# A linear recurrence with two expert mixtures: the recurrence's maskings and scalings regrouped, the masked logits on another engine

## The chip, the cores and the metric

The kernel runs on one core of a Trainium2 chip. The metric is the time of one execution in microseconds (us). The core has five engines that work side by side: TensorE (PE, matrix products; its weight loads are listed as PEld), VectorE (DVE), ScalarE (ACT), GpSimd (POOL) and SyncE (SP, which here only issues DMAs). They wait for each other by semaphores.

## The reference

Three stages follow each other. The first is a recurrence over 768 positions for 4 batches and 8 heads of 48 elements:

```python
for t in range(S):
    cur = einsum('bhd,bhe->bhde', u[None] * k[:, :, t], v[:, :, t])
    y[:, :, t] = einsum('bhd,bhde->bhe', r[:, :, t], state + cur)
    state = w[None, :, :, None] * state + einsum('bhd,bhe->bhde', k[:, :, t], v[:, :, t])
```

The second is a mixture of 8 experts over the 3072 rows of 384. Rows whose product with w_skip isn't positive pass unchanged; the others choose the expert of the largest logit, go through its two layers with a ReLU between, and are added to, weighted by the softmax of the chosen logit. The third is a soft mixture: every row has 32 logits (one per slot); a softmax over all rows gives each slot its input, each of 8 experts works on four slots, and a softmax over the slots mixes the results back into the rows.

## The kernel before

The recurrence is done in chunks. A tile is 128 positions of one batch, all 8 heads; there are 24 tiles, tile j being chunk j // 4 of batch j % 4. Heads are kept in pairs: four pairs on the free dimension, the two heads of a pair on partitions 0 to 47 and 64 to 111, hence tiles of 112 partitions by 4 x 128 columns. Tables of decays, prt for r and pkt for k (the same table read backwards), scale r and k, so that one product of the scaled k and r gives the scores within the tile; a mask leaves the past, and the diagonal (the bonus u) is put in separately.

The engines' order is written out by hand: what stands in the program is the order on each engine. A loop over i = 0 to 23 holds, in this order, scores(i), state(i-1), amask(i-1), inter(i-1), stateb(i-1), trx(i-2), prep(i+1), prepk(i+1), upd(i), bonus(i), av(i-1), and pieces of the routing between them:

- prep(j) (L612): VectorE scales r (L616) and k (L618), GpSimd makes the product pd of r and k (L620). prepk(j): GpSimd scales k for the state, kt (L626).
- scores(j): TensorE makes the scores sc (L635) and the diagonal's values dt (L638); ScalarE copies dt. bonus(j): TensorE transposes them to dtk (L657).
- state(j): GpSimd multiplies the old state by the decay, tmp (L668), VectorE adds TensorE's update up (L669). stateb(j): ScalarE spreads the state for use (L677).
- past(j) (L679): VectorE multiplies the two halves of sc (one head of each pair) by the mask (L683). amask(j) (L685): VectorE puts the diagonal into both halves, at (L691).
- inter(j): TensorE adds the state's part (L703); av(j): the scores' part (L713), ScalarE copies it to yt (L716). trx(j): TensorE transposes yt, ScalarE copies it to x (L723).
- load(j): SyncE issues r and k for the buffer rkb, and k and v for kvt, three tiles ahead.

Routing goes in groups of four tiles: GR has five groups of four, then groups of two, one and one tile. route1 makes the logits (L745), route2 transposes them, route2b and choose find the chosen expert: m is 1 for a row that is computed, oh marks the expert, and mb is 0 or 65536 (L835, L796), so that rows that pass unchanged get a place out of bounds. route3 sums up, on TensorE, the places, from eb2 (the expert's number), the counts so far (ohacc) and oh; places turns them into idx (L877). scat(j) is GpSimd's indirect DMA of one tile's rows to their places in xs_d (L891); one follows in each step from i = 8 on. route4 (L897) comes in the steps i = 8, 12, 16 and 20, behind prep and count: GpSimd copies the slots' logits to lt (L903), VectorE makes the masked ones, ltm = m * NEG + logits (L904), their maximum over the group (L906), and the maximum so far, cmax (L907). In step 21, cmax is spread for the transposition that gives the maximum of each slot over the first 16 tiles (fourfold).

The first mixture starts on gathered rows when every scatter has landed. It and the second mixture aren't touched by the change. pools: rs has three buffers, ks two, at two, pd two, sc two (PSUM), the tile of dtk one, that of up one.

Of the kernel before, what the change touches and what calls it, by code (L numbers as in the profile page):

```python
# [8 lines left out]
F32 = mybir.dt.float32  # L9
# [3 lines left out]
AF = mybir.ActivationFunctionType  # L13
ALU = mybir.AluOpType
# [24 lines left out]
class Banks:  # L39
    """PSUM tiles by role: role -> [(pool, tag, bufs)], taken in turn."""  # L40
# [12 lines left out]
class Views:  # L53
    """Tiles cut out of one flat tile whose own contents are no longer needed."""
# [53 lines left out]
class Weighted:  # L108
    """Sums of the rows weighted per slot, four tiles at a time: [(quarter, slot), columns]."""
# [24 lines left out]
def slots(nc, cn, nm, pp, tag, dsb, ss):  # L134
    """Slot inputs (transposed) and, on every partition, the slots' sums: [128, 4, 32]."""
    sib = pp.tile([P, 4, 32], F32, tag=tag, name=f"sib{nm}")
    for k in range(3):
        nc.tensor.matmul(sib[:, k, :], dsb[:, k * P : (k + 1) * P], cn["sel4"], start=(k == 0), stop=False)
    nc.tensor.matmul(sib[:, 3, :], cn["onesf"], ss, start=False, stop=True)
    return sib  # L140
# [16 lines left out]
class Rows:  # L157
    """The outputs of the slots come on four rows each, (hi | hi | lo | lo): row 32 j + 8 q + s has slot 8 j + s."""
# [19 lines left out]
# pieces of the second mixture's weights, in the order of their use: half an expert's v1, or 128 rows of v2 of four experts  # L178
# [76 lines left out]
def weights(nc, lp, ez, lt, p, cx=None):  # L255
    """The combine weights of chunks 2p and 2p + 1, columns (hi | lo | hi | lo) of eight slots each."""
# [67 lines left out]
def general(tc, cn, dp, r_in, k_in, v_in, w_in, u_in, wcn, phi, w1, w2, v1, v2, out):  # L324
# [142 lines left out]
def tile_main(ctx, tc, rk, kv, wu, wcat, phi, w1, w2, v1, v2, r_in, k_in, v_in, w_in, u_in, wcn, out, dbg=None, force=False):  # L467
# [21 lines left out]
    def warm(pool, tag, n):  # L489
        """Keeps the tensor engine busy, so that its clock is up when the work arrives."""  # L490
# [48 lines left out]
    nc.vector.tensor_scalar(eb2, eb_i, 1.0 / (E * P), None, op0=ALU.mult)  # L539
# [26 lines left out]
    nc.vector.memset(cmax, NEG)  # L566
# [21 lines left out]
    prt = kp.tile([PR, 4, P], F32, name="prt")  # L588
    nc.vector.tensor_mul(prt, pt[:, :, 0:P], iw.to_broadcast([PR, 4, P]))
    pkt = prt[:, :, ::-1]  # L590
    pktok = kp.tile([P, H, D], F32, name="pktok")

    def decays():
        """The decays of k, token-major."""
# [17 lines left out]
    def prep(j):  # L612
        t = T[j]
        rkt = t["rk"]
        t["rs"] = wk.tile([PR, 4, P], F32, tag="rs", bufs=3, name=f"rs{j}")
        nc.vector.tensor_mul(t["rs"], rkt[:, 0], prt)  # L616
        t["ks"] = wk.tile([PR, 4, P], F32, tag="ks", name=f"ks{j}")
        nc.vector.tensor_mul(t["ks"], rkt[:, 1], pkt)  # L618
# [60 lines left out]
    def past(j):  # L679
        t = T[j]  # L680
        at = t["at"] = wk.tile([P, 2, 4, P], F32, tag="at", name=f"at{j}")
        for hf in range(2):
            nc.vector.tensor_mul(at[:, hf], t["sc"][:, hf], mask.rearrange("s (o t) -> s o t", o=1).to_broadcast([P, 4, P]))  # L683

    def amask(j):  # L685
# [4 lines left out]
        for hf in range(2):  # L690
            nc.vector.copy_predicated(  # L691
                at[:, hf],
                ident_i.rearrange("s (o t) -> s o t", o=1).to_broadcast([P, 4, P]),
                t["dtk"].rearrange("s (p r) -> s p r", r=32)[:, :, hf : hf + 1].to_broadcast([P, 4, P]),
            )
# [34 lines left out]
    # maxima of the slots' logits over the groups of tiles: on every row, and a slot per partition  # L730
# [17 lines left out]
    # what the last eight tiles' groups leave behind  # L748
# [10 lines left out]
    def direct(g, tag):  # L759
        """Logits of one tile, token-major at once."""  # L760
# [9 lines left out]
    def choose(g, src):  # L770
        """The choice of one tile's tokens, step by step, by way of fewer steps than several tiles take."""
# [22 lines left out]
        yield  # L794
        mb = r["mb"] = rt.tile([P, 1, 1], F32, tag="mb", name=f"mb{g}")
        nc.vector.tensor_scalar(mb, m, -65536.0, 65536.0, op0=ALU.mult, op1=ALU.add)  # L796
# [16 lines left out]
    def route2b(g):  # L813
# [20 lines left out]
        mb = r["mb"] = rt.tile([P, nb, 1], F32, tag="mb", name=f"mb{c}")  # L834
        nc.vector.tensor_scalar(mb, m, -65536.0, 65536.0, op0=ALU.mult, op1=ALU.add)  # L835
# [32 lines left out]
    def places(g):  # L868
# [8 lines left out]
        nc.vector.tensor_add(idx[:, j0 : j0 + nb].rearrange("t (b o) -> t b o", o=1), sl, r["mb"])  # L877
# [20 lines left out]
    def route4(g):  # L898
# [5 lines left out]
        nc.vector.scalar_tensor_tensor(ltm[:, j0 : j0 + nb, :], m.to_broadcast([P, nb, 32]), NEG, lg[:, :, 9:41], op0=ALU.mult, op1=ALU.add)  # L904
        cm = rt.tile([P, 32], F32, tag="cm", name=f"cm{c}")
        nc.vector.tensor_reduce(cm, ltm[:, j0 : j0 + nb, :].rearrange("t b s -> t s b"), axis=AX.X, op=ALU.max)  # L906
        nc.vector.tensor_max(cmax, cmax, cm)  # L907
# [12 lines left out]
    class Group:  # L920
        """Maximum, exponentials and weighted sums of some tiles, in pieces for the steps' gaps."""
# [50 lines left out]
    if True:  # L972
        for i in range(NT):
# [24 lines left out]
            if i == 21:  # L998
                c4t = fourfold(nc, "t", rt, cmax)
# [73 lines left out]
        weave("ccgcpgcpgccpcc", c=choose(6, "lg"), g=gates(5), p=places(5))  # L1073
# [11 lines left out]
        weave("gggccpcpcpcccc", c=choose(7, "lgp"), g=gates(6), p=places(6))  # L1085
# [27 lines left out]
        # tokens per expert, and how many decays are within bounds  # L1113
# [36 lines left out]
    def mm1(n):  # L1150
# [3 lines left out]
        # the products that need the rows' low parts come last  # L1154
# [392 lines left out]
```

## Time and profile before

| | us |
|---|---|
| median of 3 runs | 395.06 |
| lowest and highest | 393.02, 395.08 |
| span of the profiled execution | 399.5 |

The profile gives the span of its execution, from the first to the last instruction, and no other time of it. Busy time over the span: TensorE 356.0 us (89%), VectorE 279.8 (70%), ScalarE 157.4 (39%), GpSimd 124.9 (31%). A line of a timeline has the start in us from the span's start, the duration in us, the engine, the line of the kernel, the operation, what it writes and reads (partitions x elements), how many neighbours were put together (x2), and in brackets how long the engine had been idle and what ended that. An operation of VectorE that waits for something other than a semaphore is shown as busy, so it is only seen by its length. The granted clock is a share of the full 2.4 GHz; at 0.50 it is at 1.2 GHz.

### The profile page before, as it was taken

The numbers are of one execution on the slowest core, as the hardware profiler recorded it, in microseconds if no ns is written. First come the engines' busy times: TensorE is split into PE (matmuls) and PEld (weight loads), VectorE is DVE, ScalarE is ACT, GpSimd is POOL, SyncE is SP. The second block draws the span as 40 slices with busy tenths as digits, with TensorE's granted clock in tenths as the row PEclk, the third lists the DMA queues.
The fourth block names the chain that finished last, engine by engine and source line by source line (L and its number), as shares of the span: only waits on it lengthen the run. The fifth ranks groups of instructions, "written<-read, shape, count | busy, mean of one in ns | idle before, by whom it ended". The sixth has DMA issues, their size and how long they took to land. (4 is left out here: it accounts for less than half of the span.)

```text
span 399.5 us, 8463 instructions
## 1 busy us (share of the span) xinstructions
PE 356.0 (89%) x3291; PEld 286.5 (72%) x3291; DVE 279.8 (70%) x588; ACT 157.4 (39%) x337; POOL 124.9 (31%) x147
## 2 busy tenths in 40 slices
PE   6888997997979959889999999999999999999560
PEld 2676785685756837727999999999899999734250
DVE  8899799599896996664757575757575865426360
ACT  1223442242433413344546555555465652321170
POOL 7846538367684350532002020202020202010000
PEclk9668997899998979959999999999999999999895
DMA  6999768497953410128795968787877357669575
GB/s 170 254 318 244 177 190 236 114 292 180 278 160 97 121 40 2 40 88 308 254 328 200 323 213 311 223 295 239 274 256 262 117 208 244 233 216 286 174 280 203
DMA packets 46049, 84.32 MB, mean 211 GB/s; under 512 B 4361, under 2 KB 27119, under 8 KB 46000
## 3 DMA queue, kind: packets, MB, share of 16 engines
q1 hardware_dynamic: 42336, 78.68, 63.5%
q0 software_dynamic: 2720, 4.89, 4.2%
q8 instruction: 28, 0.46, 0.5%
q10 hardware_dynamic: 944, 0.12, 0.3%
q14 instruction: 21, 0.17, 0.1%
HBM read 72.88 MB, written 13.30 MB: 216 GB/s over the span
## 5 line engine op out<-in xcount | busy, mean ns | idle before, releaser
L1157 PE MATMUL hp<-xhl,wa 128*128 128x256 f32 x192 | 48.6, 290 | 0.2 <-ACT xhl L1147 0.2
L1158 PE MATMUL hp<-xhl,wa 128*128 128x256 f32 x192 | 47.2, 282 | 0.0
L953 DVE TENSOR_TENSOR wa<-w,wa 128x768 fp32r<-128x768 f32 x32 | 30.6, 955 | 22.1 <-ACT wa L965 20.9
L1182 PE MATMUL yp<-wb,hh 128*128 128x384 f32 x128 | 45.3, 354 | 0.0
L1183 PE MATMUL yp<-wb,hh 128*128 128x384 f32 x128 | 43.1, 337 | 0.0
L1184 PE MATMUL yp<-wb,hlo 128*128 128x384 f32 x128 | 43.1, 337 | 0.0
L620 POOL TENSOR_TENSOR pd<-rkb 112x512 f32<-112x512 f32 x24 | 32.5, 1352 | 32.8 <-PE dt L638 20.2
L1215 POOL DMA_INDIRECT lt_d<-lsr,id x16 | 17.5, 1097 | 80.2 <-ACT xhl L1147 56.7
L891 POOL DMA_INDIRECT xs_d<-x,idx x24 | 26.1, 1087 | 37.5 <-ACT x L723 17.6
L1157 PEld LDWEIGHTS hp<-xhl,wa 128*128 128x128 f32 x192 | 36.4, 189 | 0.5 <-ACT xhl L1147 0.5
L1158 PEld LDWEIGHTS hp<-xhl,wa 128*128 128x128 f32 x192 | 36.5, 190 | 0.0
L635 PEld LDWEIGHTS sc<-rs,ks 48*128 48x128 f32 x384 | 25.0, 199 | 15.9 <-DVE ks L618 9.6
L635 PE MATMUL sc<-rs,ks 48*128 48x128 f32 x384 | 29.8, 298 | 6.7 <-DVE ks L618 6.7
L953 DVE TENSOR_TENSOR wb<-w,wb 128x768 fp32r<-128x768 f32 x32 | 30.6, 955 | 3.1 <-ACT wb L965 3.1
L691 DVE COPY_PREDICATED at<-ident,dtk 128x512 f32<-128x512 int32 x48 | 31.8, 715 | 0.0
L683 DVE TENSOR_TENSOR at<-sc,mask 128x512 f32<-128x512 f32 x48 | 30.6, 678 | 1.5 <-PE sc L635 1.5
L1168 DVE SCALAR_TENSOR_TENSOR hlo<-hp,hh 128x512 fp32r<-128x512 f32 x32 | 22.0, 688 | 12.4 <-ACT hh L1167 12.4
L713 PE MATMUL yp<-at,kvt 128*48 128x128 f32 (+1 forms) x384 | 30.7, 310 | 0.0
L965 ACT CAST wb<-w 128x768 fp32r<-128x768 f32 x32 | 26.8, 837 | 9.0 <-PE yp L1184 5.1
L1167 ACT ACTIVATE hh<-hp 128x512 fp32r<-128x512 f32 x32 | 19.1, 598 | 26.2 <-PE hp L1160 26.2
L1160 PE MATMUL hp<-xhl,wa 128*128 128x256 f32 x192 | 28.3, 283 | 0.0
L716 ACT COPY yt<-yp 112x512 f32<-112x512 f32 x24 | 14.0, 585 | 33.1 <-PE yp L713 33.1
(320 smaller groups left out, 747.6 us busy)
## 6 DMA issues: line engine op xcount, KB each, us to landing
w<-in_w_dram SPq DMA_DIRECT2D x32, 768.0 KB
v<-in_v_dram SPq DMA_DIRECT2D x29, 768.0 KB
rkb<-in_rk_dram SPq DMA_DIRECT2D x48, 192.0 KB
kvt<-in_kv_dram SPq DMA_DIRECT2D x24, 384.0 KB
out_dram<-ob SPq DMA_DIRECT2D x5, 768.0 KB
xs_d<-zt SPq DMA_DIRECT2D x1, 3096.0 KB
xg<-xs_d POOLq DMA_DIRECT2D x6, 387.0 KB, 4.5
x<-in_v_dram SPq DMA_DIRECT2D x2, 768.0 KB
```

What stands on the lines that cost most here:

```text
L620: nc.gpsimd.tensor_mul(t["pd"], rkt[:, 0], rkt[:, 1])
L635: nc.tensor.matmul(sc[:, hf, p, :], ks[r0 : r0 + D, p, :], rs[r0 : r0 + D, p, :], start=True, stop=True)
L683: nc.vector.tensor_mul(at[:, hf], t["sc"][:, hf], mask.rearrange("s (o t) -> s o t", o=1).to_broadcast([P, 4, P]))
L691: nc.vector.copy_predicated(at[:, hf], ident_i.rearrange("s (o t) -> s o t", o=1).to_broadcast([P, 4, P]), t["dtk"].rearrange("s (p r) -> ...
L713: nc.tensor.matmul(yp[64 * hf : 64 * hf + m, p, :], kvt[:, 1, h * D : h * D + m], at[:, hf, p, :], start=(c == 0 and p == 0), stop=(p == 3))
L953: nc.vector.tensor_sub(lv, sl, hv.bitcast(F32))
L1157: nc.tensor.matmul(hp[:, f, :], hi[:, k, fs], xh[:, k, :], start=(k == 0 and f == 0), stop=False)
L1158: nc.tensor.matmul(hp[:, f, :], lo[:, k, fs], xh[:, k, :], start=False, stop=False)
L1160: nc.tensor.matmul(hp[:, f, :], hi[:, k, fs], xl[:, k, :], start=False, stop=(k == 2 and f == 1))
L1182: nc.tensor.matmul(YP[e][bl], hh[:, f, bs], hi[:, f, :], start=st, stop=False)
L1183: nc.tensor.matmul(YP[e][bl], hh[:, f, bs], lo[:, f, :], start=False, stop=False)
L1184: nc.tensor.matmul(YP[e][bl], hlo[:, f, bs], hi[:, f, :], start=False, stop=en)
```

## The change

Five things are done otherwise:

- The masked logits are made by ScalarE: one scaling of m by NEG for the group, and for each of its four tiles an addition of a bias per row. The group's maximum and the running maximum go; in step 21 VectorE takes one maximum over the 16 tiles.
- The tables prt and pkt stand in one tile, prk (the reversed one is copied there once), and one VectorE operation scales r and k, into one tile with three buffers.
- The mask is one VectorE operation over both halves, and so is the diagonal.
- mb goes: eb2 has the expert's number on partition 0 and -65536 / 8 on partition 32, which the product with a matrix of 8 adds to each chosen place; places then adds 65536 to all.
- The orders of the two weaves at the end have one step less for it; cmax needs no initial value.

The core of the diff (removed comments, empty lines and the steps of the weaves left out):

```diff
@@ constants
-    nc.vector.tensor_scalar(eb2, eb_i, 1.0 / (E * P), None, op0=ALU.mult)
+    nc.gpsimd.memset(eb2, 0.0)
+    nc.vector.tensor_scalar(eb2[0:1], eb_i[0:1], 1.0 / E, None, op0=ALU.mult)
+    nc.vector.memset(eb2[32:33], -float(NOROW // E))
-    nc.vector.memset(cmax, NEG)
@@ decay tables
-    prt = kp.tile([PR, 4, P], F32, name="prt")
+    prk = kp.tile([PR, 2, 4, P], F32, name="prk")
+    prt, pkt = prk[:, 0], prk[:, 1]
     nc.vector.tensor_mul(prt, pt[:, :, 0:P], iw.to_broadcast([PR, 4, P]))
-    pkt = prt[:, :, ::-1]
+    nc.vector.tensor_copy(pkt, prt[:, :, ::-1])
@@ def prep(j)
-        t["rs"] = wk.tile([PR, 4, P], F32, tag="rs", bufs=3, name=f"rs{j}")
-        nc.vector.tensor_mul(t["rs"], rkt[:, 0], prt)
-        t["ks"] = wk.tile([PR, 4, P], F32, tag="ks", name=f"ks{j}")
-        nc.vector.tensor_mul(t["ks"], rkt[:, 1], pkt)
+        rks = wk.tile([PR, 2, 4, P], F32, tag="rks", bufs=3, name=f"rks{j}")
+        t["rs"], t["ks"] = rks[:, 0], rks[:, 1]
+        nc.vector.tensor_mul(rks, rkt, prk)
@@ def past(j)
-        for hf in range(2):
-            nc.vector.tensor_mul(at[:, hf], t["sc"][:, hf], mask.rearrange("s (o t) -> s o t", o=1).to_broadcast([P, 4, P]))
+        nc.vector.tensor_mul(at, t["sc"], mask.rearrange("s (a o t) -> s a o t", a=1, o=1).to_broadcast([P, 2, 4, P]))
@@ def amask(j)
-        for hf in range(2):
-            nc.vector.copy_predicated(
-                at[:, hf],
-                ident_i.rearrange("s (o t) -> s o t", o=1).to_broadcast([P, 4, P]),
-                t["dtk"].rearrange("s (p r) -> s p r", r=32)[:, :, hf : hf + 1].to_broadcast([P, 4, P]),
-            )
+        nc.vector.copy_predicated(
+            at,
+            ident_i.rearrange("s (a o t) -> s a o t", a=1, o=1).to_broadcast([P, 2, 4, P]),
+            t["dtk"].rearrange("s (p o r) -> s r p o", o=1, r=32)[:, 0:2].to_broadcast([P, 2, 4, P]),
+        )
@@ choose, route2b
-        nc.vector.tensor_scalar(mb, m, -65536.0, 65536.0, op0=ALU.mult, op1=ALU.add)
@@ def places(g)
-        nc.vector.tensor_add(idx[:, j0 : j0 + nb].rearrange("t (b o) -> t b o", o=1), sl, r["mb"])
+        nc.vector.tensor_scalar(idx[:, j0 : j0 + nb].rearrange("t (b o) -> t b o", o=1), sl, float(NOROW), None, op0=ALU.add)
@@ def route4(g)
-        nc.vector.scalar_tensor_tensor(ltm[:, j0 : j0 + nb, :], m.to_broadcast([P, nb, 32]), NEG, lg[:, :, 9:41], op0=ALU.mult, op1=ALU.add)
-        cm = rt.tile([P, 32], F32, tag="cm", name=f"cm{c}")
-        nc.vector.tensor_reduce(cm, ltm[:, j0 : j0 + nb, :].rearrange("t b s -> t s b"), axis=AX.X, op=ALU.max)
-        nc.vector.tensor_max(cmax, cmax, cm)
+        mn = rt.tile([P, nb, 1], F32, tag="mn", name=f"mn{c}")
+        nc.scalar.mul(mn, m, NEG)
+        for b in range(nb):
+            nc.scalar.activation(ltm[:, j0 + b, :], lg[:, b, 9:41], AF.Identity, bias=mn[:, b, :])
@@ the loop over i
             if i == 21:
+                nc.vector.tensor_reduce(cmax, ltm[:, 0:16, :].rearrange("t b s -> t s b"), axis=AX.X, op=ALU.max)
                 c4t = fourfold(nc, "t", rt, cmax)
```

## Rows read from the trace of the kernel before

**Rows 1.** Busy time by window: us, TensorE, loads, VectorE, ScalarE, GpSimd, clock, DMA, GB/s.

```profile
20.00:30.00 10.00, 8.91 (x102) 7.21 (x103) 10.00 (x14) 2.54 (x7) 4.92 (x5) 0.66 1.04 317
67.00:70.00 3.00, 3.00 (x21) 2.19 (x22) 3.00 (x6) 0.59 (x1) 1.78 (x2) 0.50 0.46 113
200.00:300.00 100.00, 100.00 (x734) 95.64 (x733) 63.80 (x103) 54.63 (x103) 16.18 (x20) 1.00 0.79 266
```

**Rows 2.** Timeline of TensorE, recurrence: start, us, line, operation, count, idle before, releaser.

```profile
38.14 1.20 PE L635 MATMUL sc<-rs,ks 48*128 48x128 f32 x16
...
44.65 1.16 PE L635 MATMUL sc<-rs,ks 48*128 48x128 f32 x16
...
60.17 1.16 PE L635 MATMUL sc<-rs,ks 48*128 48x128 f32 x16
...
66.76 0.47 PE L657 MATMUL dtk<-ident,dts 128*128 128x128 f32 x1 [1.77 <-DVE at L691]
...
72.45 1.16 PE L635 MATMUL sc<-rs,ks 48*128 48x128 f32 x16
...
87.95 1.16 PE L635 MATMUL sc<-rs,ks 48*128 48x128 f32 x16
...
97.38 1.16 PE L635 MATMUL sc<-rs,ks 48*128 48x128 f32 x16
...
112.88 1.16 PE L635 MATMUL sc<-rs,ks 48*128 48x128 f32 x16
...
124.01 1.16 PE L635 MATMUL sc<-rs,ks 48*128 48x128 f32 x16
...
138.85 1.16 PE L635 MATMUL sc<-rs,ks 48*128 48x128 f32 x16
...
146.19 0.47 PE L657 MATMUL dtk<-ident,dts 128*128 128x128 f32 x1 [4.39 <-DVE at L691]
...
151.53 1.16 PE L635 MATMUL sc<-rs,ks 48*128 48x128 f32 x16
```

**Rows 3.** Timeline of VectorE from 59 to 66 us.

```profile
59.43 3.65 DVE L904 SCALAR_TENSOR_TENSOR ltt<-m,lg 128x128 f32<-128x128 f32 x1
...
63.92 0.34 DVE L669 TENSOR_TENSOR sp<-up,tmp 112x192 f32<-112x192 f32 x1
...
64.19 1.27 DVE L683 TENSOR_TENSOR at<-sc,mask 128x512 f32<-128x512 f32 x2
...
65.39 1.32 DVE L691 COPY_PREDICATED at<-ident,dtk 128x512 f32<-128x512 int32 x2
```

**Rows 4.** Timeline of GpSimd from 58 to 63 us.

```profile
58.87 1.33 POOL L891 DMA_INDIRECT xs_d<-x,idx  x1 [3.09 <-ACT sbd L677]
...
61.94 0.99 POOL L626 TENSOR_TENSOR kt<-kvt,pktok 128x384 f32<-128x384 f32 x1
```

**Rows 5.** Timeline of VectorE behind the recurrence.

```profile
173.11 0.42 DVE L1097 SCALAR_TENSOR_TENSOR ltt<-m,lg 128x256 f32<-128x256 f32 x1
173.57 0.58 DVE L1098 TENSOR_REDUCE cmax<-ltt 128x32 f32<-128x256 f32 x1
```

**Rows 6.** Groups by line and form, ScalarE, 0 to 185 us: busy us, mean ns.

```profile
L829 ACT ACTIVATE ex<-dd 128x32 f32<-128x32 f32 x5 | 1.1, 229 | 0.9 <-DVE dd L825 0.8
```

**Rows 7.** Groups by line and form, VectorE, 0 to 170 us.

```profile
L583 DVE TENSOR_TENSOR pt<-pt 112x256 f32<-112x256 f32 x1 | 0.4, 424 | 0.0
...
L583 DVE TENSOR_TENSOR pt<-pt 112x128 f32<-112x128 f32 x1 | 0.3, 291 | 0.0
```

**Rows 8.** Timeline of VectorE, early steps.

```profile
24.23 2.71 DVE L618 TENSOR_TENSOR ks<-rkb,prt 112x512 f32<-112x512 f32 x1
```

**Rows 9.** Timeline of TensorE, early steps.

```profile
21.09 2.02 PE L635 MATMUL sc<-rs,ks 48*128 48x128 f32 x16 [2.31 <-DVE ks L618]
...
32.95 1.16 PE L635 MATMUL sc<-rs,ks 48*128 48x128 f32 x16 [1.35 <-DVE ks L618]
```

**Rows 10.** Timeline of VectorE in a step that chooses experts.

```profile
52.28 1.11 DVE L835 TENSOR_SCALAR mb<-m 128x4 f32<-128x4 f32 x1
```

More of the change, by code (lines that the diff above doesn't have):

```diff
@@ L794, in choose @@
         yield
-        mb = r["mb"] = rt.tile([P, 1, 1], F32, tag="mb", name=f"mb{g}")
-        nc.vector.tensor_scalar(mb, m, -65536.0, 65536.0, op0=ALU.mult, op1=ALU.add)
-        yield
         oh = r["oh"] = rtile(g, "oh", oh8, BF16)
@@ L833, in route2b @@
         nc.vector.tensor_reduce(m2, t8, axis=AX.X, op=ALU.max)
-        mb = r["mb"] = rt.tile([P, nb, 1], F32, tag="mb", name=f"mb{c}")
-        nc.vector.tensor_scalar(mb, m, -65536.0, 65536.0, op0=ALU.mult, op1=ALU.add)
         oh = r["oh"] = rtile(g, "oh", oh8, BF16)
@@ L1072, in tile_main @@
         route3(5, "t", (4,))
-        weave("ccgcpgcpgccpcc", c=choose(6, "lg"), g=gates(5), p=places(5))
+        weave("ccgcpgcpgcpcc", c=choose(6, "lg"), g=gates(5), p=places(5))
         for j in range(20, 22):
@@ L1084, in tile_main @@
         trx(23, "tp", pc)
-        weave("gggccpcpcpcccc", c=choose(7, "lgp"), g=gates(6), p=places(6))
+        weave("gggccpcpcpccc", c=choose(7, "lgp"), g=gates(6), p=places(6))
         nc.scalar.copy(RT[7]["lg"], RT[7]["lgp"][:, :, 0:42])
```

## The prediction

> **What bounds the kernel now.** I read the stages first (busy time by window, [rows 1]), then TensorE's timeline through the recurrence [rows 2], and then, for each hole in it, VectorE's timeline [rows 3] and GpSimd's [rows 4] at the same moment. The chain of waits on the page has one piece and says nothing here. From 200 to 300 us TensorE is busy for all 100 us at full clock (the first mixture): nothing that this change touches is in there, so whatever the recurrence gives is a plain shift of that stage. In the recurrence (about 9 to 170 us) VectorE fills whole windows, 10.00 of 10.00 us from 20 to 30, where the granted clock is 0.66, that is partly at the lower of its two levels (1.2 GHz).
>
> [rows 2] gives the step from one tile's scores to the next. Every fourth step also carries the logits of a group. Where nothing disturbs it, at 38.14 to 44.65, such a step takes 6.51 us. The three steps after it take 60.17 - 44.65 = 15.52, or 5.17 each. The next fourth steps take 72.45 - 60.17 = 12.28, 97.38 - 87.95 = 9.43, 124.01 - 112.88 = 11.13 and 151.53 - 138.85 = 12.68 us. These four are where the time is lost. At 66.76 TensorE has waited 1.77 us for VectorE's diagonal (L691), at 146.19 it has waited 4.39; and behind the first hole the clock is down to 0.50 (67 to 70 us, [rows 1]), the lower level, so that the products after it take twice as long.
>
> The cause stands in [rows 3] and [rows 4]. At the end of each group, route4 masks the logits on VectorE (L904). That operation starts at 59.43 and lasts 3.65 us; with the maximum and the running maximum behind it (L906, L907), VectorE gets to the state update only at 63.92, 4.49 us later. The same operation at twice the width, 128x256, takes 0.42 us at 173.11 [rows 5], behind GpSimd's last product. So it isn't work, it is a wait: GpSimd begins a scatter at 58.87 and runs without a gap to the end of the kt product, 61.94 + 0.99 = 62.93, and L904 ends 0.15 us behind that. The Trainium skill, "SBUF — State Buffer", section "Who interferes with whom", has a VectorE instruction with two SBUF inputs and a GpSimd instruction that reads SBUF exclude each other, for the length of one instruction. By that rule L904 would have waited for the scatter alone, 1.33 us, and taking it away would be worth about 1 us a group; the trace shows the wait through four GpSimd operations in a row, and I go by the trace.
>
> **Part 1, the masked logits.** Four times, L904, L906 and L907 go: 4.49 us of VectorE at the first. In their place ScalarE does one small scaling and four additions with a bias per row, 128x32 each. The nearest row is the exponential of 128x32, 0.23 us [rows 6]; five in a train are 0.9 to 1.3 us. They stand behind ScalarE's copy of x and ahead of its copy of yt, which waits for TensorE then; their inputs were made a step earlier. If that cover were gone they would put off yt by at most 1.3 us, which the logits' products would see. I cost them at 0. (The Trainium skill, "ScalarE: Activation LUTs", section "Rules for kernel authors", speaks against the move: additions and products belong on VectorE, which is faster per element. By it the sum would be a loss of some 1 us of ScalarE a group; here what matters is who waits for GpSimd, and the 0.23 us of [rows 6] hold no such wait.) With the wait gone, what is late next? The state update needs GpSimd's tmp product, which lies behind the scatter, between 60.20 and 61.94: VectorE goes on near 60.8 (an estimate) rather than 63.92, 3.1 us earlier. Mask (1.20 us, from 64.19 to 65.39) and diagonal (as much) then end near 63.3, when TensorE has just come to the transposition that waited until 66.76. So the hole closes, and with it the loss of clock. The first three fourth steps become 6.51 us: 5.77 + 2.92 + 4.62 = 13.3 us.
>
> **The fourth of them is different.** Here the one maximum over 16 tiles stands ahead of the mask on VectorE, and waits for ScalarE's last addition. In place of the first group's 4.49 us stand a wait of about 1.0 us for the additions and a maximum of 128x512 of about 1.0 us (0.58 at 128x256, [rows 5], in proportion to columns less a fixed part): 2.5 us earlier. If the clock stays up as well it is more; 12.68 - 6.51 = 6.2 is the most. If the copy behind the maximum (SBUF to SBUF, no row shows it beside GpSimd) waits as long as L904 did, some 3.4 us, nothing is left. I take 3.8, between 2.5 and 6.2, since the clock was down behind the first hole as well; ends 0 and 6.2.
>
> **Part 2, r and k scaling in one operation, mask and diagonal in one each.** Work saved: for a product of two tensors 256 columns cost 0.424 and 128 cost 0.291 us [rows 7], so 1.04 ns a column and 0.16 fixed, of which neighbours overlap about half: 0.06 to 0.08 us per merged pair, three pairs a step, 0.2 us. Where TensorE sets the pace that is worth nothing; between 12 and 40 us, where VectorE does, 6 steps, 1.2 us. More comes from the waits. The scaling of r and k has two SBUF inputs. The scaling of k at 24.23 takes 2.71 us [rows 8] for what is some 0.65 of work (half of the pair at 64.19, [rows 3]): it waits for GpSimd, while that of r, just ahead, got in. One operation can wait once, not twice, and starts where r's started. Against that, it holds GpSimd for twice as long, and the products pd and kt start up to 0.6 us later; they are needed a step later. TensorE waited 2.31 us for the scaling at 21.09 and 1.35 at 32.95 [rows 9], with the clock down in between. Bounds: 0 (each wait only moves) to 4.5 us (both holes and the merges). Above that the DMA would set the pace: its share is 1.04 from 20 to 30 us [rows 1], so the r and k of later tiles can't land much earlier. I take 3.0, nearest to the two holes less one wait that stays.
>
> **Part 3, small ones.** The copy of the reversed decay table adds an operation of 112x512 ahead of the first scaling: 0.3 to 0.7 us, partly beside the wait for GpSimd's first product: 0.3 lost. The constant row for the slot (mb) goes; at 52.28 it takes 1.11 us [rows 10], again a wait for GpSimd. The next operation with two SBUF inputs is the merged scaling, which takes that wait over: 0, at most 1.0 a group. And in the three closed holes the merged scaling comes at about 63.3, when GpSimd has ended kt (62.93) and goes on to the next scatter: if it is caught behind a run of GpSimd as L904 was, the next scores are late by some 1.3 us. I take 0.8 for all of that, at most 4.5.
>
> **Sum.** 13.3 + 3.8 + 3.0 - 0.3 - 0.8 = 19.0 us. The profile gives its execution's span, 399.5 us, and no time apart from it; the median of the runs is 395.06, 1.1% less, which would make 19.0 into 18.8. I subtract 19.0 from the median: 376.0 us.
>
> **Rivals.** (a) *The wait moves rather than goes.* The merged scaling inherits it at all four ends of groups and in the early steps: 13.3 - 4.5 + 0 + 0 - 0.3 = 8.5 us, 386.5 us. For it: the scaling is the next operation with two SBUF inputs, and GpSimd has the same work to do. Against it: in the closed holes it comes 3 us ahead of need. (b) *Slower: the wait comes in every step.* The merged scaling is long, GpSimd is late by it, runs without gaps to catch up, and so catches the next scaling. VectorE's work of a step is 1.20 + 1.20 + 1.2 + 0.3 (63.92 to 64.19) = 3.9 us against 5.17 of TensorE, so up to 1.27 us of waiting a step is hidden; from there it decides. With 3.4 us, as L904's, in each of the 12 steps from 60.17 to 138.85: (3.4 - 1.27) x 12 = 25.6 lost against 19.0 won, 401.7 us. Against it: GpSimd has gaps in most steps now. (c) *No change*: the shift is given back before the first mixture, for instance if the gathered rows wait for something that isn't moved: within 2 us of 395. Against it: the scatters follow the steps. (d) *More than I count*: the clock stays up from the first scores on, and 6.2 in the fourth: 13.3 + 6.2 + 4.5 = 24.0, 371.0 us.
>
> **Numbers.** My forecast with its own bounds 0.73, (a) 0.13, (d) 0.07, (c) 0.03, (b) 0.04. The range that holds 8 in 10 goes from (d)'s 371.0 to 384.0, between the forecast and (a). A measurement of this kernel can tell about 0.5% (2 us) from no change; so faster 0.93, same 0.03, slower 0.04.
>
> **What would show it.** Right: no VectorE operation of route4 left; the four fourth steps at 6.5, 6.5, 6.5 and under 10 us; TensorE's clock at 1.00 from 60 to 125 us; ScalarE's additions of 0.2 to 0.3 us, done before yt's copy would wait; the first mixture starting 17 to 21 us earlier with its own length unchanged. Wrong: merged scalings of over 1.3 us (a wait on GpSimd) in more than a few steps, GpSimd's pd or kt stretched so that TensorE waits for them, TensorE waiting for ScalarE's yt, or a diagonal or mask that costs more per column merged than split.

## The result and the profile after

| | before | after |
|---|---|---|
| median, us | 395.07 (4 runs) | 380.75 (4 runs) |
| lowest and highest, us | 393.02, 398.72 | 379.41, 381.62 |
| span of the profiled execution, us | 399.5 | 379.9 |
| ratio of the times, 95% interval | | 0.9654, 0.9604 to 0.9705 |

The change makes the kernel 14.3 us faster by the medians; 19.0 was forecast (376.0 us, measured 380.75, inside the range of 371.0 to 384.0). The spans differ by 19.6, which looks like the sum of the prediction and isn't, as the part on the reasons shows. Three executions, one of before (811.8 us), one of e5 (535.33) and one of e11 (811.76), took far longer than all the others, and the ratios leave such slow ones out.

TensorE's timeline through the recurrence, of the kernel after; columns as in [rows 2], whose steps these lines answer:

```profile
35.90 1.16 PE L636 MATMUL sc<-rks 48*128 48x128 f32 x16
42.37 1.16 PE L636 MATMUL sc<-rks 48*128 48x128 f32 x16
47.71 1.16 PE L636 MATMUL sc<-rks 48*128 48x128 f32 x16
...
50.75 0.43 PE L639 MATMUL dt<-pd,usel 112*32 112x128 f32 x8 [1.87 <-DVE lg L814]
...
56.23 1.16 PE L636 MATMUL sc<-rks 48*128 48x128 f32 x16
60.98 1.16 PE L636 MATMUL sc<-rks 48*128 48x128 f32 x16
67.45 1.16 PE L636 MATMUL sc<-rks 48*128 48x128 f32 x16
...
83.04 1.16 PE L636 MATMUL sc<-rks 48*128 48x128 f32 x16
89.51 1.16 PE L636 MATMUL sc<-rks 48*128 48x128 f32 x16
...
105.63 1.16 PE L636 MATMUL sc<-rks 48*128 48x128 f32 x16
113.68 1.16 PE L636 MATMUL sc<-rks 48*128 48x128 f32 x16 [1.18 <-DVE rks L619]
...
128.80 1.16 PE L636 MATMUL sc<-rks 48*128 48x128 f32 x16
136.88 1.16 PE L636 MATMUL sc<-rks 48*128 48x128 f32 x16
```

The fourth steps are 6.47, 6.47, 8.05 and 8.08 us, where [rows 2] gives 12.28, 9.43, 11.13 and 12.68: the four holes are gone or halved. There is another hole in an ordinary step: from tile 7's scores at 47.71 to tile 8's at 56.23 (called step 7 to 8 from here on) it takes 8.52 us, where the profile of before that the prediction read has 5.43. It isn't the change's own: a second profile of before has it too (e0).

Busy time by window, kernel after (columns as in [rows 1]):

```profile
51.00:54.70 3.70, 3.70 (x36) 3.24 (x28) 2.67 (x6) 1.56 (x5) 1.26 (x1) 0.54 0.38 80
67.00:70.00 3.00, 3.00 (x38) 2.23 (x35) 2.90 (x3) 0.85 (x2) 2.81 (x3) 1.00 1.04 250
200.00:300.00 100.00, 100.00 (x732) 95.64 (x731) 65.14 (x108) 54.76 (x104) 16.08 (x20) 1.00 0.75 251
```

From 67 to 70 us the granted clock is 1.00, not 0.50 as in [rows 1]. The clock now falls behind the hole of step 7 to 8: 0.54 from 51.0 to 54.7 us, close to the lower level. The first mixture is what it was, TensorE busy all the time.

What took the place of the masking operation is in ScalarE's timeline and its groups by line and form (busy us, mean ns), kernel after:

```profile
60.08 0.21 ACT L899 ACTIVATE mn<-m 128x4 f32<-128x4 f32 x1
60.32 0.96 ACT L901 ACTIVATE ltt<-lg,mn 128x32 f32<-128x32 f32 x4
61.19 0.56 ACT L715 COPY yt<-yp 112x512 f32<-112x512 f32 x1
...
L901 ACT ACTIVATE ltt<-lg,mn 128x32 f32<-128x32 f32 x16 | 3.8, 310 | 0.1
```

1.1 us, ahead of the copy of yt, and no line of TensorE waits for that copy here. [rows 3] had 3.65 us in L904 alone.

### The profile page after: what moved, and what is told of

It is laid out like the page before. It is cut to its first block, busy times and chain, and to the rows that moved or that the text cites. A ratio compares the mean times of both kernels' runs of the same rounds, so it can differ in the third digit from the quotient of the medians.

```text
span 379.9 us, 8387 instructions
## 1 busy us (share of the span) xinstructions
PE 346.0 (91%) x3291; PEld 282.4 (74%) x3291; DVE 264.6 (70%) x498; ACT 161.9 (43%) x357; POOL 127.7 (34%) x148
## 5 line engine op out<-in xcount | busy, mean ns | idle before, releaser
L619 DVE TENSOR_TENSOR rks<-rkb,prk 112x1024 f32<-112x1024 f32 x24 | 37.6, 1567 | 0.0
L885 POOL DMA_INDIRECT xs_d<-x,idx x24 | 27.3, 1138 | 29.6 <-ACT x L722 11.2
L621 POOL TENSOR_TENSOR pd<-rkb 112x512 f32<-112x512 f32 x24 | 31.3, 1304 | 15.4 <-DMA rkb<-in_rk_dram 7.3
L636 PE MATMUL sc<-rks 48*128 48x128 f32 x384 | 29.7, 297 | 6.0 <-DVE rks L619 6.0
L636 PEld LDWEIGHTS sc<-rks 48*128 48x128 f32 x384 | 24.9, 199 | 13.5 <-DVE rks L619 8.3
L690 DVE COPY_PREDICATED at<-ident,dtk 128x1024 f32<-128x1024 int32 x24 | 31.4, 1310 | 2.3
L683 DVE TENSOR_TENSOR at<-sc,mask 128x1024 f32<-128x1024 f32 x24 | 29.1, 1213 | 0.0
L712 PE MATMUL yp<-at,kvt 128*48 128x128 f32 (+1 forms) x384 | 27.0, 283 | 0.0
## 6 DMA issues: line engine op xcount, KB each, us to landing
kvt<-in_kv_dram SPq DMA_DIRECT2D x24, 384.0 KB, 6.1
xs_d<-zt SPq DMA_DIRECT2D x1, 3096.0 KB, 14.3
```

Of the source, the lines that this page charges most:

```text
L619: nc.vector.tensor_mul(rks, rkt, prk)
L621: nc.gpsimd.tensor_mul(t["pd"], rkt[:, 0], rkt[:, 1])
L636: nc.tensor.matmul(sc[:, hf, p, :], ks[r0 : r0 + D, p, :], rs[r0 : r0 + D, p, :], start=True, stop=True)
L683: nc.vector.tensor_mul(at, t["sc"], mask.rearrange("s (a o t) -> s a o t", a=1, o=1).to_broadcast([P, 2, 4, P]))
L690: nc.vector.copy_predicated(at, ident_i.rearrange("s (a o t) -> s a o t", a=1, o=1).to_broadcast([P, 2, 4, P]), t["dtk"].rearrange("s (p o ...
```

## The experiments

The experiments were measured in three sets, each on one chip beside before, and the sets differ: before came out at 400.7, 395.3 and 397.2 us (medians). So ratios are compared within a set. The first set has e0 to e3, the second e4 to e7, the third e8 to e11. Expectations of e0 to e3 that are given in microseconds were made for a before of 395; against them a ratio times 395.07 is what counts.

**e0: the kernel before once more.** No edit. It tells how far two runs of the same program come apart.

> The kernel before, unchanged, profiled once more. Question: was the execution whose rows the prediction used a typical one? Its span was 399.5 us at a mean clock of 0.924, against a median time of 395.07. If it was typical, the span here is again over 398 us with the four fourth steps near 12.3, 9.4, 11.1 and 12.7 us. If it was a slow one, because the clock stayed low behind some of the holes by chance, the span is 392 to 394 us, the clock higher, and fourth steps are nearer to 9.4 each.

Measured: 399.69 us, ratio 0.9919 (0.9867 to 0.9970). The same program twice, and the interval leaves 1 out, though the medians of all executions, 399.69 and 400.70, are 0.3% apart: here anything within 0.8% is no difference. The span is 399.0 us, and the fourth steps are 11.25, 9.42, 11.13 and 12.57 us: the four holes are in both profiles of before.

Ahead of them the two profiles differ. From the first scores to those of tile 6 e0 takes 32.34 us (9.29 to 41.63), the profile that the prediction read 35.35 (9.30 to 44.65). And step 7 to 8 is 7.19 us in e0, not 5.43 (GpSimd and TensorE, e0):

```profile
36.92 1.28 POOL L620 TENSOR_TENSOR pd<-rkb 112x512 f32<-112x512 f32 x1 [5.44 <-DMA rkb<-in_rk_dram]
...
50.26 0.42 PE L638 MATMUL dt<-pd,usel 112*32 112x128 f32 x8 [2.12 <-DVE lg L818]
```

GpSimd waits 5.44 us for r and k there, against 0.44 in the first profile, the test of the weights (three operations on wt) is caught (0.96 and 0.43 us, free 0.17 and 0.16), and TensorE waits 2.12 us for VectorE's lg. So the unchanged kernel can be 3 us faster early on, and can have the hole of step 7 to 8. e1 and e7, which don't merge the scaling either, agree with e0 in both: tile 6 at 41.0 and 40.4 us, step 7 to 8 of 8.55 and 8.85 us.

**e1: the logits alone.** Of the change only the masked logits and the one maximum:

```diff
-        nc.vector.scalar_tensor_tensor(ltm[:, j0 : j0 + nb, :], m.to_broadcast([P, nb, 32]), NEG, lg[:, :, 9:41], op0=ALU.mult, op1=ALU.add)
...
+        nc.scalar.mul(mn, m, NEG)
+        for b in range(nb):
+            nc.scalar.activation(ltm[:, j0 + b, :], lg[:, b, 9:41], AF.Identity, bias=mn[:, b, :])
```

> Only the masked logits move to ScalarE, with the one maximum over 16 tiles; scalings, mask, diagonal and mb stay as before. Theory 1 (the gain is the four holes that VectorE's wait for GpSimd makes): 380 to 384 us, the first three fourth steps at 6.5 us. Rival (the gain is mostly fewer VectorE operations and waits in the early steps): 388 us or more.

Measured: 387.70 us, ratio 0.9673 (0.9616 to 0.9730); fourth steps 6.96, 7.37, 7.35 and 9.60 us. This one part carries the gain of the whole change (0.9654 in its own measurement), and the ratio times 395.07 is 382.1, inside theory 1. The steps aren't quite 6.5: VectorE's scaling of k, still an operation of its own, is held for 3.17 or 3.18 us behind each of the first three ends of groups (63.39, 86.59, 109.78), and TensorE waits 0.4 to 0.8 us for it.

**e2: the merges alone.** The scaling, the mask and the diagonal in one operation each, logits as before.

> Only the merges: one scaling of r and k, one mask, one diagonal, with the table of the reversed decays copied; the masked logits stay on VectorE. Theory 1: 391 to 395 us, the holes stay at 9 us or more, the early steps give 0 to 3 us. Rival (fewer operations): 387 us or less.

Measured: 400.69 us, ratio 0.9960 (0.9916 to 1.0005): nothing that can be told from no change, though 3.0 us (0.9925) would still lie within the interval. The fourth steps keep their holes (8.02, 9.49, 11.16, 12.63 us). The trace says where an early gain went. The early steps are in fact shorter, tile 5's scores start at 29.3 us against 35.2 in e0. Then VectorE and TensorE wait (their timelines, e2):

```profile
36.93 1.23 DVE L618 TENSOR_TENSOR rks<-rkb,prk 112x1024 f32<-112x1024 f32 x1 [5.07 <-DMA rkb<-in_rk_dram]
...
44.78 2.19 DVE L1055 TENSOR_SCALAR wok<-wt 112x4 f32<-112x4 f32 x1
...
50.81 0.66 PE L638 MATMUL dt<-pd,usel 112*32 112x128 f32 x8 [4.10 <-DVE lg L816]
```

The transfers of r and k hold the run up (5.07 us), a VectorE operation on 112x4 is held for 2.19 us, TensorE waits 4.10 us, and step 7 to 8 takes 11.98 us. At tile 8 e2 is at 57.5 us, e0 at 54.2.

**e3: the masking operation, but earlier.** Kernel before, with the counts and route4 ahead of the scaling instead of behind it:

```diff
+            if rok and rb == 3:
+                count(rc)
+                route4(rc)
...
-            if rok and rb == 3:
-                count(rc)
-                route4(rc)
```

> The kernel before with count and route4 ahead of the scaling in their step, all on VectorE as before. Theory 1 (VectorE waits because GpSimd is in a run of its own at that moment, not because of the work): L904 takes 0.2 to 0.4 us instead of 3.5, the holes close, 382 to 387 us. Rival (these operations on VectorE are the cost wherever they stand): no change, 394 to 396 us. A third outcome: the scaling, now later, takes over the wait, and the gain is half, 388 to 391.

Measured: 402.16 us, ratio 0.9995 (0.9953 to 1.0038). VectorE's and GpSimd's timelines, e3:

```profile
55.93 0.28 DVE L904 SCALAR_TENSOR_TENSOR ltt<-m,lg 128x128 f32<-128x128 f32 x1
57.38 3.61 DVE L618 TENSOR_TENSOR ks<-rkb,prt 112x512 f32<-112x512 f32 x1
...
56.59 1.13 POOL L891 DMA_INDIRECT xs_d<-x,idx  x1 [3.33 <-ACT sbd L677]
59.45 0.98 POOL L626 TENSOR_TENSOR kt<-kvt,pktok 128x384 f32<-128x384 f32 x1
```

The masking operation is 0.28 us of work, as the prediction said of [rows 3]. But the 3.6 us stay: the scaling of k, which now comes at that time, is held until GpSimd's run ends with kt at 60.43. The wait belongs to the time and not to the operation, and it moved whole. Rival (a) is what this kernel does.

**e4: the kernel after with the scaling split again.**

```diff
-        nc.vector.tensor_mul(rks, rkt, prk)
+        nc.vector.tensor_mul(t["rs"], rkt[:, 0], prt)
+        nc.vector.tensor_mul(t["ks"], rkt[:, 1], pkt)
```

> The kernel after, with the scaling of r and k split again into two VectorE operations (mask, diagonal and logits stay as in after). Theory 1 (a merged scaling waits once where two wait twice, but in the presence of the other parts it costs as much as it gives): within 2 us of after's ratio of 0.965, so 0.960 to 0.971; the early scalings wait in the k half again (2.5 to 3 us at about 24), and the one wait of 4.35 us at 109 goes, its step falling from 8.05 to about 6.5 us, or shows up as a wait of k's half alone. Theory 2 (the merge is worth the 3.0 us that the prediction gave the early steps): ratio 0.970 to 0.975. Theory 3 (the long scaling is what stretches GpSimd and costs more than it gives): ratio 0.955 to 0.960.

Measured: 386.16 us (382.73 to 388.90), ratio 0.9804 (0.9723 to 0.9885). By the time this is above every expectation, and it can't be set against a run of after, which wasn't in this set; the time settles nothing. By the steps the two are even: tile 23 starts at 141.9 us, in after at 141.8. Split, the first three ends of groups take 7.50, 7.40 and 7.37 us, some 0.9 to 1.0 more than the undisturbed 6.47, and step 7 to 8 takes 2.8 less than in after (5.68). As in e1, the half for k is held behind each of those ends (3.17 to 3.19 us at 63.83, 87.16 and 110.47), where the merged scaling is held once in after (4.35 us for 1.2) and by 0.26 us at most in e8. So with the logits moved, the merged scaling saves some 0.9 us at an end of a group in these profiles; the times don't resolve it.

**e5: after, weights' test late.** The test, three operations on wt (L1052, L1054, L1056 of after), goes from step 6 to step 22.

> The kernel after, with the three one-time VectorE operations on the weights (the test of wt, 0.99 to 1.24 us each in after at 45 to 47 us) moved from step 6 to step 22. If they are what makes step 7 to 8 last 8.52 instead of 5.43 us in after: that step falls to 5.2 to 5.6 us, TensorE no longer waits 1.87 us at 50.75, the clock stays at 1.00 from 50 to 55 us, and the ratio falls by 2 to 3 us against after's 0.965, to 0.956 to 0.960. If instead the transfers of r and k set the pace there (the scaling of tile 6 waited for them at 36.9): the step falls but the next ones grow by the same amount, ratio 0.963 to 0.967. If the wait for GpSimd only moves to the next operation with two inputs, the step stays above 7.5 us.

**e6: e5 with the scatters one step later.**

```diff
-            if 8 <= i < 24:
-                scat(i - 8)
-        for j in range(16, 20):
+            if 9 <= i < 24:
+                scat(i - 9)
+        for j in range(15, 20):
```

> As the kernel before this one (weights late), with each GpSimd scatter put one step later, so that its slot indices have long been made and GpSimd does not stand waiting for them and then run four operations without a gap. If the waits of VectorE come from these runs without gaps: the wait of 4.35 us at the scaling at 109 and that of oh (1.01 us, three times) go, the fourth steps are 6.5, 6.5, 6.5 and 8.0 us, and the time is 1.5 to 4 us below the kernel with the weights late alone. If they come from the amount of GpSimd's work, wherever it stands: no difference (within 1 us), and merged scalings of over 2 us at other places from 45 to 140 us.

Measured: e5 380.06 us, ratio 0.9634 (0.9574 to 0.9694); e6 376.88, ratio 0.9555 (0.9506 to 0.9604). In e5 step 7 to 8 stays at 8.26 us, in e6 it is 5.52; behind tile 8 they are alike (83.2 and 83.5 us to tile 23). So my first reading of the hole fell: with the weights' test away it is still there, the wait having moved to the scaling. And the later scatter brings nothing once the masking has left VectorE: up to step 7 no scatter has been issued in either, so the 2.7 us aren't its doing. The waits of oh (1.01 us, four times) stay in e6, where they were to go. Where the two profiles part is in these rows (VectorE and GpSimd at one moment, first e5, then e6):

```profile
43.90 2.33 DVE L619 TENSOR_TENSOR rks<-rkb,prk 112x1024 f32<-112x1024 f32 x1
...
43.87 1.27 POOL L621 TENSOR_TENSOR pd<-rkb 112x512 f32<-112x512 f32 x1
```

```profile
43.63 1.21 DVE L619 TENSOR_TENSOR rks<-rkb,prk 112x1024 f32<-112x1024 f32 x1
...
43.65 2.33 POOL L621 TENSOR_TENSOR pd<-rkb 112x512 f32<-112x512 f32 x1 [0.17 <-POOL tmp L669]
```

In e5 GpSimd is first, by 0.03 us, and VectorE's scaling lasts 2.33 us instead of 1.21. In e6 VectorE is first, by 0.02 us, and GpSimd's product lasts 2.33 instead of 1.27. GpSimd had room, VectorE had not: in e5 TensorE then waited 1.64 us for VectorE's lg. The Trainium skill, "SBUF — State Buffer", section "Who interferes with whom", says that a VectorE instruction with two SBUF inputs contends with a GpSimd instruction that reads SBUF, and that the order of issue, not the shape of the operation, decides who blocks. These two pairs agree with it.

**e7: the kernel before with the scatters one step later**, the diff of e6 on the kernel before.

> The kernel before, with the logits still masked on VectorE, and only the scatters put one step later. Theory 1 (the masking operation is held through GpSimd's run without gaps, which begins at the scatter that waited for its indices): the masking operation falls from 3.65 to 0.3 to 1.5 us at most of the four ends of groups, the first three fourth steps come to 6.5 to 8 us, and the time falls by 6 to 12 us (ratio 0.970 to 0.985) without moving anything to ScalarE. Rival (it is held by whatever GpSimd does there, mostly tmp, pd and kt): still 2.5 us or more, fourth steps of 9.4 us or more, ratio 0.992 to 1.000. Third outcome (the wait moves to the scaling behind, as in the kernel with the logits early): masking short, but a scaling of over 3 us and the same time as before.

Measured: 382.49 us, ratio 0.9696 (0.9637 to 0.9755), as much as e1 gives in its set. All uses of L904, first in before, then in e7 (ns: shortest, median, longest), and then two lines of GpSimd in e7:

```profile
L904 DVE SCALAR_TENSOR_TENSOR ltt<-m,lg x4: 2106/3520/3652, 59.4 to 138.9; 128x128 f32<-128x128 f32 x4
```

```profile
L904 DVE SCALAR_TENSOR_TENSOR ltt<-m,lg x4: 279/464/643, 59.6 to 129.3; 128x128 f32<-128x128 f32 x4
...
58.32 1.32 POOL L626 TENSOR_TENSOR kt<-kvt,pktok 128x384 f32<-128x384 f32 x1 [0.75 <-POOL pd L620]
59.82 1.13 POOL L891 DMA_INDIRECT xs_d<-x,idx  x1 [0.18 <-issue]
```

Where [rows 4] has GpSimd idle 3.09 us ahead of the scatter and then busy without a gap for four operations, here the scatter has its indices from the step before, GpSimd is done with kt at 59.64, and L904 at 59.59 meets only its end. The fourth steps are 7.13, 7.22, 7.22 and 6.95 us. Nothing was taken from VectorE: the holes were made by GpSimd's late start at the scatter, and they go by either cure.

**e8: the kernel after once more**, no edit, to have it on the chip of the last three.

> The kernel after, unchanged, beside the next three on one chip. Its span was 379.9 us in its first profile against 399.5 of before in another session: 19.6, where the medians differ by 14.3. If the gain is 14 us and the profile of before lay above its median: ratio 0.960 to 0.967. If it is what the spans show, 19 us: 0.950 to 0.956. Its profile should again show first scores near 10.5 us, step 7 to 8 over 8 us, and one or more scalings of over 3 us behind 45 us.

Measured: 386.02 us, ratio 0.9751 (0.9672 to 0.9829), gain 11.2 us by the medians; a smaller gain than in the first measurement, and above both ranges of the expectation. The recurrence is the same to a tenth: tile 23 at 141.8 us in both profiles of after. Two things within it differ: the third fourth step is 6.47 (8.05), step 7 to 8 is 10.63 (8.52). No scaling behind 45 us is held for over 3 us, though one was expected. And behind the recurrence the stretch from tile 23's scores to the first mixture takes 24.0 us (20.5).

**e9: after with the scatters one step later**, the weights' test staying.

> The kernel after with only the scatters one step later; the weights' test stays in step 6. By the runs so far (weights late 0.9634, both 0.9555): if the scatter alone makes the difference, 0.953 to 0.960, step 7 to 8 under 6 us, no scaling of over 3 us behind 45 us, all fourth steps but the last under 6.7. If both moves are needed, 0.960 to 0.965, with step 7 to 8 at 8 us or more.

Measured: 383.71 us, ratio 0.9681 (0.9590 to 0.9773), step 7 to 8 9.79 us: the second outcome by that step. The ratio lies above both ranges, as that of e8 does, and the two intervals overlap. From tile 8 to tile 23 it takes 83.9 us, e8 83.4. This agrees with e5 and e6: the later scatter adds nothing to the moved logits.

**e10: e6 with the set-up of eb2 in step 1 on VectorE; e11: e10 with the zero fill issued at step 4 instead of step 2.**

```diff
-    nc.gpsimd.memset(eb2, 0.0)
-    nc.vector.tensor_scalar(eb2[0:1], eb_i[0:1], 1.0 / E, None, op0=ALU.mult)
-    nc.vector.memset(eb2[32:33], -float(NOROW // E))
...
+            if i == 1:
+                nc.vector.memset(eb2, 0.0)
+                nc.vector.tensor_scalar(eb2[0:1], eb_i[0:1], 1.0 / E, None, op0=ALU.mult)
+                nc.vector.memset(eb2[32:33], -float(NOROW // E))
```

> The kernel with weights late and scatter later, and the set-up of eb2 (a memset on GpSimd and two VectorE operations ahead of the first tile) moved to step 1 on VectorE. In after the first scores start 1.25 us later than before. If the added memset does that (the one of rkb stands behind it on GpSimd, beside the first copy of VectorE): first scores at 9.3 to 9.8 us, 0.7 to 1.2 us less than the kernel with both moves, unless the r and k transfers give it back by 45 us. If the reversed decay table does it (the prk product of 112x512, 1.66 us): first scores stay at 10.3 us or later and the time is the same.

> The kernel before this one with the zero fill of the gathered rows' buffer (3.1 MB written) issued at step 4 instead of 2. If DMA bandwidth sets the pace from 10 to 40 us, as the scaling of tile 6 waiting for rkb at 36.9 us shows in two kernels: the early steps are 0.5 to 2 us ahead at sc6 and stay so, 1 to 2 us less. If the clock and the GpSimd waits set it: the same within 1 us. If the fill is then late for the first scatter: a wait of GpSimd at the first scatter, 1 us or more lost.

Measured: e10 383.11 us, ratio 0.9645 (0.9552 to 0.9738); e11 380.21, ratio 0.9591 (0.9513 to 0.9668). The first scores start at 9.5 us in both, against 10.5 or 10.6 in e6, e8 and e9: the 1 us is the doing of eb2's set-up, of which the memset and the two operations of VectorE were moved together. VectorE and GpSimd in the kernel after, and then in e10:

```profile
4.18 0.92 DVE L581 COPY pt<-wclip 112x4 f32<-112x4 f32 x1
...
4.13 2.75 POOL L608 MEMSET rkb<- 32x1024 f32 x3
```

```profile
3.92 0.17 DVE L578 COPY pt<-wclip 112x4 f32<-112x4 f32 x1
...
4.08 2.72 POOL L605 MEMSET rkb<- 32x1024 f32 x3
```

A copy of 112x4 that comes 0.05 us behind the first of GpSimd's three memsets lasts 0.92 us, ahead of it 0.17. GpSimd's memset starts only 0.05 us later in after than in e10, VectorE's copy 0.26 us. But the 1 us is not kept. (Of the profile of e10, whose execution took 388.19 us, I use only the first 60 us, and no span.) It is at tile 2 at 16.0 us, where after is at 21.4, and at tile 8 at 54.8: its steps 5 to 8 are 7.00, 7.54 and 8.50. The windows of e10 and then of e11 say what stands in between:

```profile
20.00:30.00 10.00, 7.59 (x121) 5.99 (x122) 9.79 (x9) 3.55 (x10) 7.72 (x7) 1.00 1.04 316
30.00:40.00 10.00, 9.37 (x118) 6.62 (x120) 5.48 (x6) 4.00 (x9) 2.44 (x2) 1.00 1.06 259
```

```profile
20.00:30.00 10.00, 6.55 (x102) 4.98 (x100) 9.79 (x9) 3.58 (x9) 7.17 (x8) 1.00 0.71 181
30.00:40.00 10.00, 8.93 (x134) 7.07 (x134) 9.79 (x9) 3.80 (x10) 6.69 (x7) 1.00 1.05 319
```

In e10 the DMA engines are full (1.04, 1.06), and from 30 to 40 us VectorE is busy for 5.48 of 10 us and GpSimd for 2.44: they wait for tiles. GpSimd's line at the end of that wait, in e10:

```profile
37.56 2.29 POOL L618 TENSOR_TENSOR pd<-rkb 112x512 f32<-112x512 f32 x1 [9.41 <-DMA rkb<-in_rk_dram]
```

In e11 the share is 0.71 from 20 to 30 us; from there to 40 us VectorE and GpSimd are busy for 9.79 and 6.69 us, neither waits for rkb, step 7 to 8 is 5.81 us, and tile 8 starts at 52.4. Between the times of e10 and e11 the intervals overlap, so the 2.9 us are likely and not proven. Against after, e8 in the same set, e11 is 5.8 us shorter (ratios to before 0.9591 and 0.9751, intervals just apart): it beats both kernels. Whether e6 does as well can't be told, since after wasn't in its set; by the profiles it does, with the zero fill still early: tile 8 at 52.4 us in both, tile 23 at 135.9 in e6 and 136.4 in e11.

## Why the prediction was right, and where its sum was off

Gain by its own steps, from the starts of the scores in the profiles (us). The first two columns of results are against the profile that the prediction read, the repeat being e8; the last one is after against e0, the second profile of before:

| step of the sum | predicted | after | repeat | after, against e0 |
|---|---|---|---|---|
| first three fourth steps | 13.3 | 11.85 | 13.4 | 10.8 |
| the fourth | 3.8 | 4.6 | 4.6 | 4.5 |
| early steps, to tile 6 | 3.0 | 3.5 | 3.5 | 0.5 |
| step 7 to 8 | none | -3.1 | -5.2 | -1.3 |
| set-up | -0.3 | -1.25 | -1.2 | -1.3 |
| scaling caught, other steps | -0.8 | -1.0 | -0.5 | -1.0 |
| recurrence, to tile 23 | 19.0 | 14.7 | 14.7 | 12.2 |

**The cause was right.** [rows 3] was read as a wait for GpSimd's run of [rows 4], and e3 (0.28 us of work), e7 (0.28 to 0.64 us when the run is elsewhere) and e1 (the whole gain) show it. (When L904 starts, at 59.43, only 0.77 us of the scatter's 1.33 are left, so a wait for the scatter alone would have been 0.77 us and not the 1.33 that I gave. The reading stays the same.) The closed holes came out at 6.47 us, 6.51 being forecast, with the clock at 1.00 behind them, and ScalarE's additions cost 0.31 us each and delayed nothing at the first three ends. The rule that additions belong on VectorE (the Trainium skill, "ScalarE: Activation LUTs", "Rules for kernel authors") would have kept them there; e1's 3.3% says that who else wants the ports came first here. The fourth fourth step went as argued: VectorE's maximum over 16 tiles takes 1.06 us behind a wait of 0.97 for ScalarE, and the copy behind it, which might have been held, took 0.23.

**The step that failed is Part 2's 3.0 us for the early steps.** Two things in it were wrong. The first is what it was measured from: the waits of [rows 8] and [rows 9] are those of one execution. At tile 6 it stands at 44.65 us, the latest of all fourteen profiles; the others have 38.2 to 43.8, among them e0 (41.63), and e1, e3 and e7, which merge nothing (41.02, 42.20, 40.42). So the 3.5 us in the table are mostly the difference between two executions of before, and against e0 0.5 are left. What the merges give early in the whole change isn't settled; alone (e2) they brought tile 5 to 29.3 us, and it didn't last.

The second is what is late next. I saw the ceiling, the DMA share of 1.04 in [rows 1], and took it for a bound of the gain; I didn't ask what happens to a run that reaches it. GpSimd stops for the transfers (4.94 us in after, 5.44 in e0, where nothing is merged, 0.44 in the profile that I read), VectorE less, and then GpSimd works off its operations with hardly a gap, which is just what holds VectorE. GpSimd and VectorE of the kernel after:

```profile
37.21 1.28 POOL L621 TENSOR_TENSOR pd<-rkb 112x512 f32<-112x512 f32 x1 [4.94 <-DMA rkb<-in_rk_dram]
...
44.39 1.92 POOL L621 TENSOR_TENSOR pd<-rkb 112x512 f32<-112x512 f32 x1 [0.30 <-DMA rkb<-in_rk_dram]
46.35 1.00 POOL L627 TENSOR_TENSOR kt<-kvt,pktok 128x384 f32<-128x384 f32 x1
...
45.10 1.24 DVE L1052 TENSOR_SCALAR wok<-wt 112x4 f32<-112x4 f32 x1
46.37 0.99 DVE L1054 SCALAR_TENSOR_TENSOR wok<-wt,wok 112x4 f32<-112x4 f32 x1
```

Two operations on 112x4, 0.17 and 0.16 us in before, take 2.23; lg is late, TensorE waits 1.87 us, its clock falls to 0.54, and the step is 3.1 us longer than the 5.43. e0 (7.19 us, the clock at 1.00 behind its wait), e1 (8.55), e2 (11.98), e5 (8.26), e7 (8.85) and e9 (9.79) have the hole as well, some with the weights' test caught and some with a scaling: the place matters and not the operation, and neither the merges nor the moved logits are needed for it. e11, with the transfers out of the way, has 5.81. That is one profile, and e3 came to 5.61, e4 to 5.68 and e6 to 5.52 with the zero fill still early, so the hole isn't certain in any of them; that the transfers are its first cause is likely and not shown.

**Smaller terms.** Set-up: I counted the added copy (0.43 us here) and left out that eb2's set-up puts VectorE's first copy behind the start of GpSimd's memset (e10, e11: 1 us). The scalings: the wait I took to pass to the merged scaling went there once, at a price I had as L904's:

```profile
109.28 4.35 DVE L619 TENSOR_TENSOR rks<-rkb,prk 112x1024 f32<-112x1024 f32 x1
...
108.80 1.02 POOL L885 DMA_INDIRECT xs_d<-x,idx  x1 [0.16 <-issue]
109.84 0.52 POOL L669 TENSOR_TENSOR tmp<-sp,pt 112x192 f32<-112x192 f32 x1
...
111.54 0.99 POOL L627 TENSOR_TENSOR kt<-kvt,pktok 128x384 f32<-128x384 f32 x1
```

It cost TensorE 1.18 us and the third fourth step 1.6, in one of the two profiles of after. On the other side of that term stands what I didn't count, the 0.5 to 1.0 us that a split scaling loses at an end of a group (e1, e4). The wait of mb [rows 10] went to oh (1.01 us at 51.63), which comes ahead of the scaling and which I had overlooked, without harm; no run takes mb away alone. Rival (b), the wait in every step, didn't come: the median of the 24 merged scalings is 1.226 us. Rival (a) was true of e3; at the ends of groups the wait passed to the scaling whole once in after, and in e1 and e4, with the scaling split, at a price of 0.5 to 1.0 us a step.

**The spans agree with the sum by chance.** Of the 19.6 us between them, 14.7 are the recurrence. 6.5 are the stretch from the last scores to the first mixture (27.0 us in before, where the clock is 0.50 from 171 to 181 us; 20.5 in after), and 1.6 are lost at the end. The 6.5 can't be put down to the change: the same program, after, has 20.5 and 24.0, and the length goes with the set more than with the kernel. It is 24.4 to 27.4 in the four profiles of the first set (e0 27.0, e1 24.4), 20.5 to 21.1 in those of the second (e7, with its masking on VectorE, 21.1), and 23.9 to 25.5 in e8, e9 and e11 of the third. By the medians of the first measurement the gain is 14.3. What makes that stretch long or short isn't settled. One row each, ScalarE's copy of yt in after and in e8, whose input TensorE had begun at 148.93 and 148.92 (1.08 us) in the two:

```profile
150.06 0.59 ACT L715 COPY yt<-yp 112x512 f32<-112x512 f32 x1 [0.68 <-PE yp L712]
```

```profile
151.61 0.58 ACT L715 COPY yt<-yp 112x512 f32<-112x512 f32 x1 [1.88 <-PE trp L721]
```

In e8 it starts 1.55 us later; TensorE's line behind it waits for it, and the clock falls (0.76 from 151 to 156 us). The trace shows nothing that ScalarE waited for just then: the product named in the row had ended at 150.86.

## What to carry to other kernels

An operation that took ten times what the same line takes elsewhere (3.65 us against 0.28) was a wait here: find what the other engine does from its start to its end, and ask why that engine is busy there. Moving the victim to an engine that isn't held (e1) and moving the culprit's late start (e7) were worth the same here, each against before in its own set, and the traces of e6 and e9 show no more from both together; moving the victim in time (e3) was worth nothing.

A gain ahead of a stage that another resource limits should be written down as zero, not as up to the ceiling: the run that arrives early stops, and what it catches up with can cost more than it won. And take a gain from the steps that the change touches: a difference of two spans has in it whatever else differed. The same holds of the waits that a prediction prices: profile the kernel before twice, and price those that are in both (here the four holes were, and 3 us of the early waits weren't).

## What the runs showed of the hardware

**Hundredths of a microsecond decided.** By the recorded starts, 0.03 us of GpSimd's lead cost VectorE 1.1 us in e5, and 0.02 us of VectorE's lead cost GpSimd as much in e6; 0.05 us did it in the set-up.

**Waiting doesn't give the next turn.** In after the scaling at 109.28 came 0.48 us behind the start of a scatter of 1.02 us, and was held for three more operations of GpSimd (above). In e8, the same program, it came just as far behind a scatter just as long:

```profile
110.52 1.46 DVE L619 TENSOR_TENSOR rks<-rkb,prk 112x1024 f32<-112x1024 f32 x1
...
110.04 1.02 POOL L885 DMA_INDIRECT xs_d<-x,idx  x1 [0.17 <-PE yp L702]
111.09 1.25 POOL L669 TENSOR_TENSOR tmp<-sp,pt 112x192 f32<-112x192 f32 x1
```

There VectorE got in ahead of GpSimd's tmp, took 1.46 us, and tmp was the one held (1.25 us, 0.52 otherwise). So here a waiting VectorE operation got in behind the first of GpSimd's operations once and not the other time, 1.46 against 4.35 us. What decides it the traces don't show.

**Operations on 112x4 were held like large ones** (L1052: 1.24 us in after, 2.19 in e8, 0.17 free in before): the length of a held operation says nothing of its size.
